# A dilated-attention and GEGLU kernel: weighted values in adjacent pairs, exponentials in PSUM, FFN norm statistics on ScalarE, and another order

## The chip, the cores and the metric

The kernel runs on one core of a Trainium2 chip. The metric is the device time of one execution in microseconds (us); less is better. A core has five engines that run side by side, each through its own list of instructions in the order in which they were written: TensorE (PE, with PEld for its weight loads), VectorE (DVE), ScalarE (ACT), GpSimd (POOL) and SyncE (SP, which here only starts DMAs). An instruction waits on semaphores for what other engines have to finish first, and whatever stands behind it on its engine waits with it.

## The reference

Two layers, each an attention block and a feed-forward block with a layer norm ahead of each, on 2048 positions of 512 channels. The two layers share their weights.

```python
x = A_x                                   # (1, 2048, 512)
for layer in range(2):
    x = x + attention(layernorm(x), wqkv, wo)
    x = x + ffn(layernorm(x), w_gate, w_up, w_down)

def attention(x, wqkv, wo):               # 32 heads of 16 channels
    q, k, v = split(x @ wqkv)
    idx = pos - 2 * arange(8)             # 8 positions, every second one backwards
    logits = q . k[idx] / 4               # masked where idx < 0
    return (softmax(logits) . v[idx]) @ wo

def ffn(x, w_gate, w_up, w_down):         # 1792 hidden channels
    return (gelu(x @ w_gate) * (x @ w_up)) @ w_down
```

## The kernel before

**Tiles and stages.** Since every second position is attended, even and odd positions never meet inside an attention block. The 2048 positions are cut into eight chunks of 256 positions of one parity, and each layer passes over the eight chunks, 16 chunk passes in all. For a chunk, `attention_inputs` norms the rows and makes q, k and v on PE (four projections of 24 matmuls each, line 1016), sends them to DRAM (`qkvd`), and `attention` fetches them back so that each partition holds two positions (`J` = 2) and the seven before them. Attention itself is vector work, for four groups of eight heads (`hg`), which are taken in two halves of two groups (`NG` = 2). fp32 accuracy is kept by splitting each operand into two fp16 parts and running three matmuls for each product.

**Attention on DVE.** For each head group, `prod` takes q times the eight attended keys (line 1100, 2048 products for each partition), line 1109 sums them over the 16 channels of a head into the logits `lg`. For each half, the maximum over the window is taken and subtracted (lines 1131, 1136), ACT takes the exponential in place in `lg` (line 1141), and the sum, its reciprocal and the scaling follow (lines 1146, 1150, 1155). Then, for each head group, `prod` takes the weights times the attended values (line 1166), in the order position, window place `w`, channel `c`, and line 1176 sums over the window:

```python
nc.vector.tensor_reduce(o.tile(), prod.rearrange("p j w c -> p j c w"), axis=AX.X, op=ALU.add)
```

The sum over `w` is the innermost one, so this instruction reads one 4-byte word and then jumps by 128 words (512 bytes) for the next. The result `o` (one buffer) is split on ACT and POOL (lines 931, 935) and transposed by a DMA into `ot` (one buffer).

**Feed-forward.** `feed_forward` multiplies `ot` by `wo` on PE (line 979, 24 matmuls of 512 columns), adds the residual on DVE (line 1214) and norms the rows: `norm` takes mean and variance on DVE (`bn_stats` and `bn_aggr`, lines 855 and 859), POOL makes scale and bias out of them in eight small instructions (lines 909 to 921), ACT applies them (line 968). After the split and the DMA transpose into `bx`, seven **units** follow. A unit is 48 gate and up matmuls into one of two PSUM buffers `pg` (line 979, weights `w_g` and `w_u`), a gelu on ACT (line 1267), a product on DVE (line 1275), three sums on POOL (lines 1286 to 1288), a cast on ACT (line 1296), a difference on POOL (line 1301), and then a **down unit** of 21 matmuls into the PSUM accumulator `pd` (line 1310). `down` uses the seven-product form of a 2x2 block multiplication, so `pd` holds seven blocks of 256 columns; after the seventh unit, DVE gathers them into the residual (line 1337, six instructions).

`pd` lies in a PSUM tile of eight such blocks, `pd_all`, four banks of two blocks each. Early in the kernel its two halves serve as two more `pg` buffers, until the nodes called `retire` take them back.

**What sets the order.** Nothing is issued in the order of the loops. Every operation is a node of a graph `g` with an engine, an assumed duration, the data that it reads and writes and a priority; `plan` places the nodes by a list schedule, and the instructions are then written in the order of their planned starts. Buffers are leased from pools (`Lease`, `Pool`), so the plan also decides which buffer a node gets. The priorities come from a table of some 70 numbers, `AT`. Semaphore waits are put in afterwards, by the layer that records the instructions, from the memory that they touch; it does not know the plan, and the plan does not know of waits that it adds for memory which two nodes merely share.

Of the kernel before, what the change touches and what calls it, by code (L numbers as in the profile page):

```python
# [13 lines left out]
ALU = mybir.AluOpType  # L14
# [38 lines left out]
    lq0=-6486.17, lq1=-3733.04, lf0=-475.32, lo=-1195.16, lf1=-292.25, ld=-286.77, pq0=-1258.2, pq1=2564.18,  # L53
    pf0=-676.71, po=-72.24, pf1=-123.32, pd=270.05, x0=-2156.6, first=54.86, tile=9.81, ahead=10.4, lead=445.97,
    norm=359.9, proj=149.42, half=24.02, row=-49.66, att=87.48, hg1=-5.5, hg2=11.94, kv=93.28, xl=185.47, gu=9.51,
    early=1, xin=225.5, wait=-0.0, zero=-300.31, dl=0, ds=0, pds=114.94, late_end=60.76, sp=1, fp=1, ng=2,
    hgk=1.38, vlag=20.87, hgv=54.57, retire=1.9, late=31.94, hold=0, dz=5, pdu=11.07, sf0=173.25, sf1=281.83,
    a1=-45.95, a2=-92.04, mx1=17.89, put=0, pt=6, fa=[0, 0], warm=7.7, xe=-394.02, mq1=-1270.4, queue=2.72,
    x1=-302.68, start=145.78, step=67.54, c1=53.56, c2=-58.19, c3=41.55, c4=-98.58, c5=152.01, c6=-107.83,
    c7=-23.55,  # L60
# [13 lines left out]
class Lease:  # L74
# [4 lines left out]
    def slots(self):  # L79

        p = self.pool
        return [i for i, h in enumerate(p.held) if h is None and self.only in (None, i)]
# [244 lines left out]
def dilated_attention_geglu(ctx: ExitStack, tc: tile.TileContext, x, wqkv, wo, wg, wu, wd, out):  # L327
# [18 lines left out]
    prod = sb.tile([P, JM, W, P], F32, name="prod")  # L346
    make_identity(nc, ident)
# [87 lines left out]
    P_lg = pool("lg", 2, [P, JM, W, AT["ng"] * HPG])  # L435
# [8 lines left out]
    P_pd = Pool("pd", [pd_all])  # L444
    P_pr = Pool("prod", [prod], fifo=False)

    for i, w in enumerate((w_g, w_u)):
        last = Lease(P_gh, only=i)
        w.raw_key = lambda k, w=w, last=last: (last, 0) if k == w.nb - 1 else (f"r{w.key}", k)
        g.add("SP", 0.001, lambda: None, w=[(last, 0)], get=[last], prio=-2000)  # L450

    retire = []
    for i in (2, 3):
        gone = Lease(P_pg, only=i, kept=True)
# [4 lines left out]
    def exponents(name, am, keys, prio):  # L459
# [3 lines left out]
        lease = Lease(P_pg)  # L463
# [227 lines left out]
    def prep_d(prio):  # L691
# [40 lines left out]
        for u in range(NU):  # L732
# [19 lines left out]
            for s in range(2):  # L752
                sc = Lease(P_sc) if s else Lease(P_bx, only=1)
# [86 lines left out]
    def norm(xs_of, prio, on="DVE", after=0.0):  # L840
# [12 lines left out]
        for j in range(J):  # L853
# [53 lines left out]
        else:  # L907

            op(lambda m, v, c: ts(c[V], v, EPS, None, op0=ALU.add), mvs, [V])
# [10 lines left out]
            op(lambda m, v, c: tt(c[HF], m, c[SC], op=ALU.mult), [SC], [HF])  # L920
            op(lambda m, v, c: ts(c[BI], c[HF], -1.0, None, op0=ALU.mult), [HF], [BI])
        return lease, lambda j: (view()[2][SC][:, j : j + 1], view()[2][BI][:, j : j + 1])

    def split_transpose(src, src_keys, nb, dst, w, get, prio, on="SP", after=()):
# [19 lines left out]
        pt = Lease(P_pg)  # L944
# [16 lines left out]
    def normed(x_of, norm_l, scale_bias, j, dst, w, get, prio, on="SP", keep=False, after=()):  # L961
        xn = Lease(P_sc) if keep else None
# [3 lines left out]
        def emit():  # L966
# [5 lines left out]
            get=[xn] if keep else [], prio=prio,  # L972
# [81 lines left out]
    def attention(l, c, T):  # L1054
# [7 lines left out]
        for first in range(0, HG, NG):  # L1062
# [23 lines left out]
            lg, mx = Lease(P_lg), Lease(P_mx)  # L1086
# [4 lines left out]
            mxb = lambda mx=mx: mx.tile().unsqueeze(2).to_broadcast([P, J, W, nh])  # L1091

            for hg in group:
# [3 lines left out]
                def qk(q=q, k=k):  # L1097
# [12 lines left out]
                        lgv()[:, :, :, heads], prod.rearrange("p j w (h d) -> p j w h d", d=DH), axis=AX.X, op=ALU.add  # L1110
# [6 lines left out]
            if t0 == 0:  # L1117
                g.add(
                    "DVE port", t_dve(nl),
                    lambda lgv=lgv, h=h: nc.vector.scalar_tensor_tensor(  # L1120
                        lgv(), lgv(), cst["s_log", h],
                        masks[J].unsqueeze(3).to_broadcast([P, J, W, nh]),
                        op0=ALU.mult, op1=ALU.add,
                    ),
                    r=[("s_log", h)], w=[(lg, 0)], prio=prio,
                )
                scale = 1.0
            sw = lambda lgv=lgv: lgv().rearrange("p j w h -> p j h w")
            g.add(
                "DVE", t_dvr(nl),  # L1130
# [302 lines left out]
```

## Time and profile before

| | |
|---|---|
| Time, median of three runs | 1322.2 us (1313.49 to 1324.21) |
| Profiled execution: time | 1320.53 us |
| Profiled execution: span from first to last instruction | 1318.7 us |
| Mean granted TensorE clock | 0.975 of full speed |
| PE busy | 1218.3 us (92%) |
| DVE busy | 1090.7 us (83%) |
| POOL busy | 799.6 us (61%) |
| ACT busy | 490.5 us (37%) |
| DMA, mean rate over the span | 133 GB/s |

The profile shows one execution. Each engine's busy time is the time in which one of its instructions was running, waits not counted. The span is 1.8 us shorter than the time of that execution, which lies 1.7 us under the median of the three runs. Lines such as L1176 are those of the kernel above; `o<-prod` says that `o` was written and `prod` read, by the program's names without buffer numbers.

### The profile page before, as it was taken

What the parts mean: (1) busy time and instruction counts of PE and PEld (TensorE: products, weight loads), DVE (VectorE), ACT (ScalarE), POOL (GpSimd) and SP (SyncE); (2) the same over time, 40 slices, a digit from 0 to 9 for tenths busy, and PEclk for the clock granted to TensorE, in tenths of its full rate; (3) what the DMA queues carried; (4) which work ended last, traced back from release to release, by engine and by line L of the source; (5) the groups of instructions that cost most, each with busy time, mean ns of one, the idle gap of its engine ahead of it and who ended that gap; (6) DMA issues with size and microseconds to landing.
All of it is one profiled execution on the core that took longest, in us unless ns stands there. A gap on an engine that the chain in (4) does not pass through costs nothing.

```text
span 1318.7 us, 23744 instructions
## 1 busy us (share of the span) xinstructions
PE 1218.3 (92%) x9722; PEld 957.6 (73%) x9722; DVE 1090.7 (83%) x964; ACT 490.5 (37%) x691; POOL 799.6 (61%) x855
## 2 busy tenths in 40 slices
PE   5689979999989999999999998989999999997997
PEld 2355548886867778687878766877888786886886
DVE  7999998899797778989889878788988997998221
ACT  5867243333332242334243324323332323333221
POOL 3334627766674747568585827766768565565543
PEclk7899989999999999999999998999999999999999
DMA  9889861335436334645436284334433434431100
GB/s 342 290 225 239 188 198 49 101 115 160 123 113 172 94 108 124 173 130 159 138 91 186 89 205 121 90 117 121 136 101 98 137 112 118 114 107 47 37 17 17
DMA packets 195789, 174.74 MB, mean 133 GB/s; under 512 B 101904, under 2 KB 162656, under 8 KB 195680
## 3 DMA queue, kind: packets, MB, share of 16 engines
q1 hardware_dynamic: 195680, 173.23, 45.2%
q8 instruction: 76, 1.25, 0.4%
q14 instruction: 33, 0.27, 0.1%
HBM read 115.87 MB, written 33.73 MB: 113 GB/s over the span
## 4 chain that ended last, share of the span: by engine, by line
PE 32%; DVE 30%; POOL 19%; issue 8%; DMA 7%; ACT 4%; SPq 1%; POOLq 0%; DVEq 0%; ACTq 0%
PE pg L979 17%; DVE o L1176 8%; PE pd L1310 8%; PE pg L1016 6%; DVE prod L1166 4%; POOL sc L1286 4%; DVE prod L1100 4%; POOL hl L935 3%; DVE x L1337 3%; DVE lg L1109 3%; POOL sc L1287 2%; POOL sc L1288 2%; POOL w_u L1301 2%; POOL w_g L1301 2%; POOL gh L1301 1%
## 5 line engine op out<-in xcount | busy, mean ns | idle before, releaser
L979 PE MATMUL pg<-bx,w_g 128*128 128x256 f16 x2688 | 331.7, 273 | 13.2 <-DVE sc L1275 13.1
L979 PE MATMUL pg<-bx,w_u 128*128 128x256 f16 x2688 | 331.0, 273 | 0.0
L979 PEld LDWEIGHTS <-w_g 128*128 128x128 f16 x2688 | 263.8, 98 | 46.2 <-issue 14.8
L979 PEld LDWEIGHTS <-w_u 128*128 128x128 f16 x2688 | 263.5, 98 | 31.0
L1016 PE MATMUL pg<-w_q,ax 128*128 128x512 f16 (+1 forms) x1536 | 264.3, 333 | 18.7 <-DMA ax<-hl 11.3
L1176 DVE TENSOR_REDUCE o<-prod 128x256 f32<-128x2048 f32 x64 | 236.9, 3702 | 18.1 <-POOL hl L935 16.8
L1016 PEld LDWEIGHTS <-ax 128*128 128x128 f16 x1536 | 152.3, 99 | 126.8 <-issue 18.1
L1275 DVE SCALAR_TENSOR_TENSOR sc<-pg,small,sc 128x512 f32<-128x512 f32 (+1 forms) x128 | 85.4, 677 | 134.1 <-ACT sc L1267 134.0
L935 POOL TENSOR_TENSOR hl<-o,hl 128x256 f16<-128x256 f32 x64 | 83.9, 1310 | 185.1 <-ACT hl L931 185.1
L1286 POOL TENSOR_TENSOR sc<-sc 128x256 f32<-128x256 f32 x112 | 122.3, 1092 | 96.3 <-DVE sc L1275 93.8
L1100 DVE TENSOR_TENSOR prod<-kv,q 128x2048 f32<-128x2048 f32 x64 | 165.0, 2577 | 3.0 <-DMA kv<-qkvd 2.7
L1166 DVE TENSOR_TENSOR prod<-kv,lg 128x2048 f32<-128x2048 f32 x64 | 163.1, 2548 | 0.6
L1109 DVE TENSOR_REDUCE lg<-prod 128x128 f32<-128x2048 f32 x64 | 145.9, 2279 | 1.0
L1267 ACT ACTIVATE sc<-pg,small 128x512 f32<-128x512 f32 (+1 forms) x128 | 79.3, 631 | 95.6 <-PE pg L979 91.8
L1310 PE MATMUL pd<-w_d,gh 128*128 128x256 f16 x798 | 97.4, 278 | 13.3 <-DVE x L1337 13.3
L1310 PE MATMUL pd<-w_d,w_u 128*128 128x256 f16 x777 | 93.7, 276 | 11.9 <-DVE x L1337 11.6
L979 PE MATMUL pg<-w_o,ot 128*128 128x512 f16 x384 | 88.4, 384 | 12.0 <-DMA ot<-hl 10.0
L1310 PEld LDWEIGHTS <-gh 128*128 128x128 f16 x798 | 79.5, 100 | 25.5 <-issue 14.5
L1288 POOL TENSOR_TENSOR sc<-sc 128x256 f32<-128x256 f32 x112 | 91.5, 817 | 8.8
L1310 PEld LDWEIGHTS <-w_u 128*128 128x128 f16 x777 | 76.9, 99 | 24.5 <-issue 12.5
L1310 PE MATMUL pd<-w_d,w_g 128*128 128x256 f16 x777 | 91.2, 272 | 3.2 <-DVE x L1337 3.1
L1301 POOL TENSOR_TENSOR gh<-sc,gh 128x896 f16<-128x896 f32 x38 | 76.5, 2014 | 28.3 <-ACT gh L1296 28.1
(111 smaller groups left out, 1347.8 us busy)
## 6 DMA issues: line engine op xcount, KB each, us to landing
kv<-qkvd SPq DMA_DIRECT2D x128, 576.0 KB, 3.9
qkvd<-sc SPq DMA_DIRECT2D x64, 384.0 KB, 3.3
q<-qkvd SPq DMA_DIRECT2D x64, 128.0 KB, 3.7
x<-in_A_x_dram SPq DMA_DIRECT2D x9, 512.0 KB, 5.0
xs<-x SPq DMA_DIRECT2D x8, 512.0 KB, 3.3
xa<-xs SPq DMA_DIRECT2D x16, 256.0 KB, 5.9
x<-xs SPq DMA_DIRECT2D x8, 512.0 KB, 4.3
xa<-in_A_x_dram SPq DMA_DIRECT2D x14, 256.0 KB, 4.1
```

The lines of the kernel that those rows point to most:

```text
L935: "POOL", t_pool(n), lambda: nc.gpsimd.tensor_sub(lo(), src(), hi()),
L979: nc.tensor.matmul(pt, a, b, start=i == 0, stop=i == n - 1)
L1016: nc.tensor.matmul(pt[:, lo:hi], a[:, i // 2, kt], part(h * KT + kt)[:, lo:hi], start=(i, kt) == (0, 0), stop=(i, kt) == (2, KT - 1),)
L1100: nc.vector.tensor_mul(prod, win, q.tile().unsqueeze(2).to_broadcast([P, J, W, P]))
L1109: lambda lgv=lgv, heads=heads: nc.vector.tensor_reduce(lgv()[:, :, :, heads], prod.rearrange("p j w (h d) -> p j w h d", d=DH), axis=AX.X, ...
L1166: nc.vector.tensor_mul(prod.rearrange("p j w (h d) -> p j w h d", d=DH), win, lg.tile()[:, :, :, heads].unsqueeze(4).to_broadcast([P, J, W ...
L1176: lambda o=o: nc.vector.tensor_reduce(o.tile(), prod.rearrange("p j w c -> p j c w"), axis=AX.X, op=ALU.add),
L1275: lambda sel=sel, h=h, pg=pg, g_of=g_of: nc.vector.scalar_tensor_tensor(g_of()[:, sel], pg.tile()[:, sel, JM * P : JM * P + N], cst["c_up" ...
L1286: tt(b[:, 4:6], b[:, 0:2], b[:, 3:4].to_broadcast([P, 2, P]), op=ALU.add)
L1288: tt(b[:, 1:3], b[:, 1:3], b[:, 0:4:3], op=ALU.subtract)
L1301: lambda blocks=blocks, gh_of=gh_of: nc.gpsimd.tensor_sub(gh_of()[:, 1], blocks(), gh_of()[:, 0]),
L1310: nc.tensor.matmul(pd.tile()[:, PD_AT[m]], gh_of()[:, a, G_AT[m]], wd_of(u, m, b), start=u == 0 and n == 0 and PD_AT[m] % 2 == 0, stop=u = ...
```

## The change

Line numbers of the changed kernel are some 32 to 36 higher: L1166 becomes L1199, L1176 becomes L1211, the exponential L1141 becomes L1173, the down unit L1310 becomes L1346.

- **Pairs.** The weighted values are written so that window places 2q and 2q+1 of a channel are neighbours (`paired`). The product is made in two instructions for each head group, one for each position `j`, and walks place pair, place in the pair, head, channel; so it writes every second word, first the even words of a stretch of 256 and then the odd ones. The sum reads two neighbouring words and then jumps by 256 words.
- **Logits** are kept with the window innermost, so the maximum reads `lg`, and the sum the exponentials, without jumps. The mask is applied in two instructions for each half instead of one.
- **Exponentials in PSUM.** ACT writes them to `ex`, one buffer, which is the eighth block of `pd_all`; the sum, the scaling in place and the weighted values read them there. Other users of the `pg` buffers than the q, k, v projections may no longer take the half of `pd_all` in which it lies (`WHOLE`).
- **FFN norm statistics on ACT.** For each of the two rows of a partition: a copy that also gives the sum, a multiplication of that sum by -1/D, and a square with that as its bias that also gives the sum of squares. POOL's list for an FFN norm is shorter by one instruction. The norms ahead of attention keep `bn_stats` on DVE.
- **Order.** Nearly all numbers of `AT` are others (`lead=445.97` becomes `lead=1721.82`, `step=67.54` becomes `step=134.57`), and some assumed durations.

```diff
+    paired = prod.rearrange("p j w c -> p j (w c)").rearrange("p j (q c t) -> p j q c t", c=P, t=2)
...
-    P_lg = pool("lg", 2, [P, JM, W, AT["ng"] * HPG])
+    P_lg = pool("lg", 2, [P, JM, AT["ng"] * HPG, W])
...
+    WHOLE = (0, 1, 2)
+    P_pe = Pool("pe", [pd_all[:, 7].rearrange("p (j h w) -> p j h w", j=JM, h=AT["ng"] * HPG)])
...
+        for j in range(J if into else 0):
...
+                lambda j=j, sums=sums, junk=junk: act(junk(), xs_of[j][1](), AF.Copy, accum_out=sums(0)),
...
+                lambda j=j, sums=sums: nc.scalar.mul(view()[1][:, j, 0:1], sums(0), -1.0 / D),
...
+                    junk(), xs_of[j][1](), AF.Square, bias=view()[1][:, j, 0:1], accum_out=view()[1][:, j, 1:2]
...
-                lambda lgv=lgv, scale=scale: nc.scalar.activation(lgv(), lgv(), AF.Exp, scale=scale),
-                r=[("s_log", h)], w=[(lg, 0)], prio=prio - 1000, table="exp",
+                lambda lgv=lgv, ex=ex, scale=scale: nc.scalar.activation(ex.tile(), lgv(), AF.Exp, scale=scale),
+                r=[("s_log", h), (lg, 0)], w=[(ex, 0)], get=[ex], prio=prio - 1000, table="exp",
...
-                    win = bass.AP(r.tensor, r.offset, [r.ap[0], [P, J], [P, W], [DH, HPG], [1, DH]])
+                    win = bass.AP(r.tensor, r.offset, [r.ap[0], [2 * P, W // 2], [P, 2], [DH, HPG], [1, DH]])
+                    by = ex.tile()[:, j, heads].rearrange("p h (q t) -> p q t h", t=2)
                     nc.vector.tensor_mul(
-                        prod.rearrange("p j w (h d) -> p j w h d", d=DH), win,
-                        lg.tile()[:, :, :, heads].unsqueeze(4).to_broadcast([P, J, W, HPG, DH]),
+                        paired[:, j].rearrange("p q (h d) t -> p q t h d", d=DH), win,
+                        by.unsqueeze(4).to_broadcast([P, W // 2, 2, HPG, DH]),
                     )
...
-                        o.tile(), prod.rearrange("p j w c -> p j c w"), axis=AX.X, op=ALU.add
+                        o.tile(), paired.rearrange("p j q c t -> p j c q t"), axis=AX.XY, op=ALU.add
...
-        nl, sb_of = norm(xt, T - 1000, "POOL" if AT["fp"] else "DVE")
+        nl, sb_of = norm(xt, T - 1000, "POOL" if AT["fp"] else "DVE", into=xns if AT["fs"] else None)
```

The rows below are the instructions of an engine as they stand in the program, each with the semaphores that it waits for (`PE_49` is raised by PE, `DVE_49` by DVE, `DMAHW...` by a DMA); a semaphore of the instruction's own engine is among them where it reads what that engine has just written.

On DVE, in the third chunk pass of the first layer, before: two head groups' weighted values (L1166) and their sums (L1176) among other work.

```order
L1155 TENSOR_TENSOR lg_108<-lg_108,mx_110 128x256
L1337 SCALAR_TENSOR_TENSOR x_90<-pd,small,x_90 128x2x256 [waits DVE_49]
L1166 TENSOR_TENSOR prod<-kv_105,lg_108 128x2048 [waits DMAHW3_49,DVE_49]
L1176 TENSOR_REDUCE o_112<-prod 128x256 [waits DVE_49,Pool_49]
L1100 TENSOR_TENSOR prod<-kv_104,q_107 128x2048 [waits DMAHW3_49,DMAHW0_49,DVE_49]
```

And after, at a like place: the scaling (L1187) and the weighted values (L1199), which read the exponentials in the tile `pd`, with a gather of `pd` (L1373) between them.

```order
L1187 TENSOR_TENSOR pd<-pd,mx_110 128x256 [waits DVE_49,PE_49]
L1199 TENSOR_TENSOR prod<-kv_104,pd 128x4x2x128 [waits DMAHW4_49,DVE_49]
L1199 TENSOR_TENSOR prod<-kv_104,pd 128x4x2x128 [waits PE_49]
L1373 SCALAR_TENSOR_TENSOR x_90<-pd,small,x_90 128x512 [waits PE_49]
L1211 TENSOR_REDUCE o_112<-prod 128x256 [waits DVE_49,Pool_49]
L1373 SCALAR_TENSOR_TENSOR x_90<-pd,small,x_90 128x2x256 [waits PE_49]
L1199 TENSOR_TENSOR prod<-kv_103,pd 128x4x2x128 [waits DMAHW1_49,DVE_49]
```

One product became two, and products and scaling now wait for PE: of these instructions and the sum of the exponentials 39 wait for a down unit, of the 32 exponentials on ACT 21 do, where before none did.

On PE, the first rows of a down unit before (`gh` is its input, made by ACT and POOL):

```order
L979 MATMUL pg_122<-bx_95,w_u 128x256
L1310 LDWEIGHTS gh [waits Activation_49]
L1310 MATMUL pd<-w_d,gh 128x256
L1310 LDWEIGHTS gh
L1310 MATMUL pd<-w_d,gh 128x256
L1310 LDWEIGHTS gh [waits Pool_49]
```

And after:

```order
L1011 MATMUL pg_122<-bx_95,w_u 128x256
L1346 LDWEIGHTS gh [waits Activation_49]
L1346 MATMUL pd<-w_d,gh 128x256 [waits DVE_49]
L1346 LDWEIGHTS gh
L1346 MATMUL pd<-w_d,gh 128x256
L1346 LDWEIGHTS gh [waits Pool_49]
```

The first matmul of the unit now waits for DVE too. Of the 2352 down matmuls 19 waited for DVE and none for ACT before, all for gathers; after, 69 wait for DVE and 7 for ACT, 62 of these for an instruction that uses the exponentials, 12 of them for one that stands at most ten instructions ahead in the program as written (30 for one at most forty ahead; a gate and up unit alone is 96).

On DVE before, behind the residual of the first chunk pass (L1214), the statistics of its FFN norm:

```order
L1214 SCALAR_TENSOR_TENSOR x_91<-pg_122,small,x_91 128x512 [waits PE_49,Activation_49]
L1214 SCALAR_TENSOR_TENSOR x_91<-pg_122,small,x_91 128x512
L855 BN_STATS nw_116<-x_91 128x6 [waits DVE_49] x2
L859 BN_AGGR nw_116<-nw_116 128x2 [waits DVE_49] x2
L1146 TENSOR_REDUCE mx_110<-lg_108 128x32 [waits Activation_49]
```

On ACT after, the same statistics for a later chunk pass, ahead of an exponential and a gelu:

```order
L859 ACTIVATE sc_101,nw_116<-x_91 128x512 [waits DMAHW4_49,DMAHW3_49,DVE_49]
L859 ACTIVATE sc_102,nw_116<-x_91 128x512 [waits DVE_49]
L868 ACTIVATE nw_116<-nw_116 128x1 [waits Activation_49] x2
L859 ACTIVATE sc_101,nw_116<-x_91,nw_116 128x512 [waits Activation_49]
L859 ACTIVATE sc_102,nw_116<-x_91,nw_116 128x512 [waits Activation_49]
L1173 ACT_TABLE_LOAD [waits DVE_49]
L1173 ACTIVATE pd<-lg_108,small 128x256 [waits PE_49]
L1303 ACT_TABLE_LOAD [waits PE_49]
```

The statistics left DVE and stand on ACT, six instructions for a chunk pass. Over the whole program ACT's table loads go from 54 to 60, and the first gate product on DVE (L1275, now L1311) has six sums over the window ahead of it instead of seven.

More of the change, by code (lines that the diff above doesn't have):

```diff
@@ L81, in slots @@
         p = self.pool
-        return [i for i, h in enumerate(p.held) if h is None and self.only in (None, i)]
+        return [i for i, h in enumerate(p.held) if h is None and (self.only is None or i in self.only)]
     def tile(self):
@@ L971, in normed @@
             "ACT", t_act(D, 2), emit, r=[x_of[0], (norm_l, 4), (norm_l, 5)], w=[key],
-            get=[xn] if keep else [], prio=prio,
+            get=[xn] if keep and not held else [], prio=prio,
         )
```

137 lines of the change are left out of this document (82 added, 55 removed).

## The prediction

> **What bounds the kernel now.** I begin with the page: the span, the engines' shares, and the chain of work that ended last.
>
> ```profile
> span 1318.7 us, 23744 instructions
> PE 1218.3 (92%) x9722; PEld 957.6 (73%) x9722; DVE 1090.7 (83%) x964; ACT 490.5 (37%) x691; POOL 799.6 (61%) x855
> ...
> PE 32%; DVE 30%; POOL 19%; issue 8%; DMA 7%; ACT 4%; SPq 1%; POOLq 0%; DVEq 0%; ACTq 0%
> PE pg L979 17%; DVE o L1176 8%; PE pd L1310 8%; PE pg L1016 6%; DVE prod L1166 4%; POOL sc L1286 4%; DVE prod L1100 4%; POOL hl L935 3%; DVE x L1337 3%; DVE lg L1109 3%; POOL sc L1287 2%; POOL sc L1288 2%; POOL w_u L1301 2%; POOL w_g L1301 2%; POOL gh L1301 1%
> ```
>
> PE is busy for 92% of the span, yet only a third of the chain lies on it: DVE and POOL hold 49% of it. The largest single DVE piece is L1176, the sum over the window, with 8%. Next, busy time by stage: the start up to the first gate matmuls, the long middle, and the end in which no attention is left.
>
> ```profile
> core 0: us, PE busy (x) PEld busy (x) DVE busy (x) ACT busy (x) POOL busy (x), PEclk, DMA share, GB/s
> 0.00:200.00 200.00, 157.94 (x904) 91.06 (x905) 184.13 (x240) 117.64 (x183) 77.53 (x120) 0.91 0.83 245
> 200.00:1200.00 1000.00, 958.04 (x7941) 779.37 (x7939) 869.35 (x682) 347.44 (x474) 662.95 (x669) 0.99 0.43 123
> 1200.00:1319.00 119.00, 102.28 (x882) 87.22 (x880) 37.18 (x43) 25.45 (x35) 59.13 (x67) 0.95 0.09 26
> ```
>
> PE stands idle for 42.1 us in the start, 42.0 in the middle and 16.7 at the end, 100.8 us in all. The change takes no matmul away, so that sum is about the most that it can gain. DVE is at 92% in the start and 87% in the middle: two engines are near their limits at once, and a cut on one of them is paid only until the other is met.
>
> **The change part by part.** The rows that price DVE's share, mean ns of one behind the busy time:
>
> ```profile
> L1176 DVE TENSOR_REDUCE o<-prod 128x256 f32<-128x2048 f32 x64 | 236.9, 3702 | 18.1 <-POOL hl L935 16.8
> L1166 DVE TENSOR_TENSOR prod<-kv,lg 128x2048 f32<-128x2048 f32 x64 | 163.1, 2548 | 0.6
> L1109 DVE TENSOR_REDUCE lg<-prod 128x128 f32<-128x2048 f32 x64 | 145.9, 2279 | 1.0
> L1214 DVE SCALAR_TENSOR_TENSOR x<-pg,small,x 128x512 f32<-128x512 f32 x32 | 22.4, 742 | 7.1 <-PE pg L979 7.1
> L855 DVE BATCH_NORM_STATS2 nw<-x 128x6 f32<-128x512 f32 x34 | 21.7, 679 | 0.0
> L1155 DVE TENSOR_TENSOR lg<-lg,mx 128x256 f32<-128x256 f32 x32 | 19.0, 592 | 0.5
> L1131 DVE TENSOR_REDUCE mx<-lg 128x32 f32<-128x256 f32 x32 | 18.6, 580 | 0.4
> L1146 DVE TENSOR_REDUCE mx<-lg 128x32 f32<-128x256 f32 x32 | 18.5, 578 | 15.2 <-ACT lg L1141 14.9
> L859 DVE BATCH_NORM_AGGREGATE nw<-nw 128x2 f32<-128x6 f32 x64 | 10.1, 173 | 0.2
> L1120 DVE SCALAR_TENSOR_TENSOR lg<-lg,small,mask 128x256 f32<-128x256 f32 x8 | 6.5, 810 | 0.0
> L704 DVE TENSOR_TENSOR w_d<-w_d 128x512 f32<-128x512 f32 x5 | 3.4, 681 | 0.0
> ...
> L1166 DVE TENSOR_TENSOR prod<-kv,lg x64: 2257/2292/3976, 92.9 to 1210.3; 128x2048 f32<-128x2048 f32 x64
> L1176 DVE TENSOR_REDUCE o<-prod x64: 3567/3704/3777, 95.5 to 1217.0; 128x256 f32<-128x2048 f32 x64
> ```
>
> The last two rows give min, median and max. From L704 (512 elements, 681 ns) and the median of L1166 (2048, 2292 ns): 1.049 ns an element and 144 ns for the instruction. L1109 fits this with neighbouring words (2279 ns). L1176 reads as many and never takes less than 3567: (3704 - 144)/2048 = 1.74 ns an element, at a jump of 512 bytes for every word. L1131 jumps by 64 bytes: (580 - 144)/256 = 1.70. So the jump costs 0.7 ns a word, and L1176 pays it in all 64 runs: it isn't waiting for another engine.
>
> - **The sum over the window (L1211)** reads two neighbours and then jumps by 256 words. No row shows such a read; the bounds are 2279 ns (L1109) and 3702 (as now). I take the lower one, since each jump now serves two words: 64 x 1.42 = -91 us.
> - **The weighted values (L1199)**: 128 instructions of 1024 elements. L1214 against L704, both 512 elements, shows 61 ns for a PSUM operand. At the full rate one takes 144 + 61 + 1024 x 1.049 = 1279 ns, two 2558 against 2548 now: +1 us. No row shows a write that steps by two words. If that costs what the jumping read costs, one takes 205 + 1024 x 1.74 = 1.99 us: +91 us. A gain under 2548 is excluded, as the elements are as many and none has ever run faster than 1.04. I take the full rate; the step is 8 bytes, while the jumps that cost are 64 and 512, but this is the least certain number here.
> - **Smaller DVE terms.** FFN statistics leave: 32 x (679 + 173) = -27 us. The maximum and the sum without jumps, 413 and 474 ns: -5 and -3. The scaling with a PSUM operand 474: -4. The mask in halves, 16 x 278 ns instead of 8 x 810: -2.
>
> Together -131 us, DVE 1091 to 960; with the dear write, 1050.
>
> [...]
>
> ACT and POOL:
>
> ```profile
> L573 ACT ACTIVATE sc<-w_d 128x512 f32<-128x512 f32 x14 | 8.6, 618 | 0.2 <-DMA qkvd<-sc 0.2
> L741 ACT ACTIVATE w_d<-w_d,small 128x512 f32<-128x512 f32 x10 | 6.4, 711 | 0.0
> L573 ACT ACTIVATION_READ_ACCUMULATOR sc<-w_d 128x1 f32 x18 | 3.4, 189 | 0.0
> L1267 ACT ACT_TABLE_LOAD x27 | 34.6, 1283 | 43.0 <-PE pg L979 32.4 <-issue 10.2
> L921 POOL TENSOR_SCALAR nw<-nw 128x2 f32<-128x2 f32 x31 | 16.1, 518 | 2.7
> ```
>
> - **FFN statistics on ACT.** A row costs 618 + 189 for the copy with its sum, some 190 for the small product (the accumulator read is the nearest row), 711 + 189 for the square with a pointer operand: 1.9 us, 61 us in all. Six more table loads make 8. ACT ends near 560 us, 42%, and no engine-time limit is near. Latency is what counts: for a chunk pass 3.8 us instead of 1.7 on DVE, less 0.5 on POOL for the instruction that goes (L921), so 1.6 us longer from residual to normed rows, 26 us over 16 passes if nothing covered it. The next rows show the cover.
>
> ```profile
> 302.04 4.71 PE L979 MATMUL pg<-w_o,ot 128*128 128x512 f16 x21 [1.01 <-DMA ot<-hl]
> ...
> 317.36 11.86 PE L1016 MATMUL pg<-w_q,ax 128*128 128x512 f16 x72
> 329.06 1.47 PE L979 MATMUL pg<-bx,w_g 128*128 128x256 f16 x12
> ```
>
> Between the output projection (ending at 306.8) and the first gate matmul of that pass, PE has 22 us of other matmuls without a gap worth naming. In the new program three to five gate-and-down pairs of the previous pass stand there. I price the statistics at 0; without that cover, 26.
>
> - **The shared bank.** This is what the change adds without saying so. The exponentials lie in the tile of the down accumulator, and the program now carries a wait both ways: a down unit waits for the last DVE or ACT instruction on the exponentials ahead of it (62 waits), and 39 DVE and 21 ACT instructions wait for a whole down unit. What it costs is bounded by the other side's duration: 1.28 us for a running product, and a down unit of 21 matmuls:
>
> ```profile
> 285.15 2.46 PE L1310 MATMUL pd<-w_d,gh 128*128 128x256 f16 x21
> ...
> PE pd L1310 <- DVE x L1337: 28.0, 16, 5.6
> DVE sc L1275 <- ACT sc L1267: 134.0, 42, 8.8
> PE pg L979 <- DVE sc L1275: 13.1, 8, 4.8
> ```
>
> On PE: from 0 to 62 x 1.28 = 79 us. PE stands in order, so gate and up matmuls queue behind a waiting down unit. Where a gate unit (5.2 us) lies between, the product should be over; 12 waits stand close behind their product, and I take 12 x 1.28 = +15 us. The kind of wait is there already: 16 waits of a down unit for gathers, 28.0 us, 1.75 each. On DVE: from 0 to 39 x 2.46 = 96 us. Behind the waiting product stand sums, queries of the next group and the gate products L1275, for which PE waits 13.1 us now. Its cover is the 131 us that DVE has just been given, so I take 0; without that cover it is 96 us on an engine as busy as before.
>
> - **The order.** Queues keep their kinds of work: SP starts the same loads, with w_d's last loads behind the first stores of q, k, v. Projections are spread singly between gate and down units instead of in blocks of two to five, and run out earlier; PE's total stays. POOL gets no new kind of work. I price this at 0 and leave it to the range.
>
> **The sum.** DVE's cut counts where it is on the chain: L1176 holds 8% of 1318.7, 105 us, and loses 1423/3702 of it, 38%: -41 us. The other 40 us of cut DVE work lie in pieces too small for the chain's list, or off it; 0, and at most -40. PE's waits give +15. Net -26: 1320.5 (the profiled execution, 1.7 under the median, well inside the spread of 10.7 of the three runs) becomes **1294 us**. The end of that case: 1271 (the waits at 0 and a part of the remaining cut paid) to 1308 (half the chain's gain lost).
>
> **The rivals.**
> 1. *The stepped write costs like a jump* (L1199), and the result is slower. DVE is then at 1050, and with the 96 us of waits above what it has now. The chain's L1166 (4%, 53 us) grows by 3.97/2.55, +29; the waits come on the path with DVE's share of the chain, 30% of 96, +29: -41 + 29 + 15 + 29 = +32, 1353 us. It decides from where DVE's total meets the old one: (1091 - 960 - 96)/128 = 0.27 us above 1.28, so at 1.55 us for one L1199. For it: L1176 and L1131 both show jumps punished; against it: the step is far smaller.
> 2. *The bank locks PE to DVE.* All 62 waits cost a product: -41 + 79, 1358 us. It decides from 41/62 = 0.66 us a wait. For it: the planner knows nothing of these waits; against it: 50 of the 62 stand farther off.
> 3. *PE and POOL take the chain over.* PE at 96% of the middle and POOL's sums, differences and their waits are as long as before; the gain on DVE is slack: 1310 to 1325.
> 4. *The pairs do not help the read*: L1211 stays near 3.7. DVE gets 40 us at most, the waits remain: 1320.5 + 15, about 1336.
> 5. *More is gained*: the whole cut is paid and waits stay small: 1320.5 - 81 = 1240, at most; 1240 to 1270.
>
> **How the numbers follow.** Forecast 0.43; rival 1: 0.17; 2: 0.08; 3: 0.17; 4: 0.05; 5: 0.10. Within 1% of 1322.2 (1309 to 1335, about what a measurement of this kernel can tell from no change) lie rival 3 and a little of 4; so faster 0.55, same 0.19, slower 0.26. The range must take in the forecast, rivals 3 and 4, the nearer part of 5 and the milder half of 1: 1255 to 1346.
>
> **What would show it.** L1211 near 2.28 us and L1199 near 1.28 (rival 1 from 1.55); DVE's busy time near 960; ACT near 560; PE's waits for L1199 in the list of waits near 15 us in all, not 80; PE idle in the middle down from 42 us; sums L1211 no longer among the first of the chain. I am wrong if the stepped write is dear, if down units wait for products by more than 0.66 us each, or if PE's idle time stays at 100 us though DVE's cut is there.

## The result, and the profile after

The changed kernel takes 1302.1 us in the median (four runs, 1299.56 to 1303.3) against 1320.0 us before: a ratio of 0.9866 (95% interval 0.982 to 0.9912), or 18 us less. The forecast was 1294 us.

The page of the changed kernel, its head and its chain:

```profile
span 1300.3 us, 23949 instructions
PE 1215.1 (93%) x9722; PEld 955.8 (74%) x9722; DVE 937.8 (72%) x972; ACT 541.5 (42%) x857; POOL 684.7 (53%) x839
...
PE 66%; DVE 16%; DMA 5%; POOL 4%; ACT 4%; issue 4%; SPq 0%; ACTq 0%; DVEq 0%; POOLq 0%
PE pg L1011 37%; PE pd L1346 18%; PE pg L1048 8%; DVE prod L1199 4%; PE pd L1048 3%; DVE o L1211 2%; DVE x L1373 2%; DVE lg L1141 1%; DVE prod L1132 1%; DVE sc L1311 1%; DVE small L564 1%; POOL hl L966 1%; DMA kv<-qkvd 1%; DMA ax<-hl 1%; DMA bx<-hl 1%
```

DVE's busy time fell by 153 us and POOL's by 115, though POOL has only 16 instructions fewer; the span fell by 18. Two thirds of the chain now lie on PE. The same stages as before, busy time by engine:

```profile
0.00:200.00 200.00, 159.74 (x905) 91.52 (x906) 163.34 (x238) 116.23 (x191) 57.15 (x118) 0.91 0.80 241
200.00:1200.00 1000.00, 964.32 (x8005) 784.66 (x8003) 755.99 (x707) 401.33 (x629) 580.37 (x667) 0.99 0.43 125
1200.00:1301.00 101.00, 91.05 (x816) 79.59 (x814) 18.47 (x27) 23.99 (x39) 47.15 (x54) 0.97 0.05 17
```

PE's idle time is 40.3, 35.7 and about 9 us, 85.2 in all (span less busy time) against 100.4 before. So the change, with its large cut on DVE, took 15 us off PE's idle time and 3 us off its busy time. The groups that the prediction priced (mean ns of one behind the busy time), and three that it did not, the first two of them of the kernel before:

```profile
L1136 DVE TENSOR_TENSOR lg<-lg,mx 128x256 f32<-128x256 f32 x32 | 28.1, 879 | 0.5
L1100 DVE TENSOR_TENSOR prod<-kv,q 128x2048 f32<-128x2048 f32 x64 | 165.0, 2577 | 3.0 <-DMA kv<-qkvd 2.7
```

```profile
L1132 DVE TENSOR_TENSOR prod<-kv,q 128x2048 f32<-128x2048 f32 x64 | 156.6, 2447 | 9.2 <-DMA kv<-qkvd 6.1 <-issue 2.2 <-DVE x L1373 0.4
L1199 DVE TENSOR_TENSOR prod<-kv,pd 128x1024 f32<-128x1024 f32 x128 | 153.0, 1218 | 31.8 <-PE pd L1346 28.5 <-ACT sc L1068 2.3
L1211 DVE TENSOR_REDUCE o<-prod 128x256 f32<-128x2048 f32 x64 | 146.1, 2282 | 18.1 <-POOL hl L966 15.2
L1168 DVE TENSOR_TENSOR lg<-lg,mx 128x256 f32<-128x256 f32 x32 | 18.0, 561 | 0.2
```

The sum over the window is at 2282 ns, the lower of its two bounds, and the product whose write steps by two words is at 1218 ns, under the 1279 that I had estimated with 1.049 ns an element. Last, what PE waited for: of its list of waits the rows in which the exponentials or a gather hold it (us in all, times, longest):

```profile
PE pd L1346 <- DVE prod L1199: 18.7, 18, 1.8
PE pd L1346 <- DVE x L1373: 8.9, 10, 1.3
...
PE pd L1346 <- ACT pd L1173: 6.0, 3, 3.2
...
PE pd L1048 <- DVE mx L1178: 4.3, 3, 2.8
PE pd L1048 <- DVE prod L1199: 2.9, 1, 2.9
...
PE pd L1346 <- DVE mx L1178: 2.2, 3, 1.3
...
PE pd L1048 <- ACT pd L1173: 0.7, 1, 0.7
...
PE pd L1346 <- DVE pd L1187: 0.4, 1, 0.4
```

Down units waited 25 times for something done to the exponentials, 27.3 us in all, and projections (L1048), which use the other buffers in that tile early in the kernel, 7.9 us more. The row of L1373 is that of the gathers.

### The profile page after: what moved, and what is told of

The parts are those of the page before. It is cut to its first block, busy times and chain, and to the rows that moved or that the text cites. A ratio compares the mean times of both kernels' runs of the same rounds, so it can differ in the third digit from the quotient of the medians.

```text
span 1300.3 us, 23949 instructions
## 1 busy us (share of the span) xinstructions
PE 1215.1 (93%) x9722; PEld 955.8 (74%) x9722; DVE 937.8 (72%) x972; ACT 541.5 (42%) x857; POOL 684.7 (53%) x839
## 4 chain that ended last, share of the span: by engine, by line
PE 66%; DVE 16%; DMA 5%; POOL 4%; ACT 4%; issue 4%; SPq 0%; ACTq 0%; DVEq 0%; POOLq 0%
PE pg L1011 37%; PE pd L1346 18%; PE pg L1048 8%; DVE prod L1199 4%; PE pd L1048 3%; DVE o L1211 2%; DVE x L1373 2%; DVE lg L1141 1%; DVE prod L1132 1%; DVE sc L1311 1%; DVE small L564 1%; POOL hl L966 1%; DMA kv<-qkvd 1%; DMA ax<-hl 1%; DMA bx<-hl 1%
## 5 line engine op out<-in xcount | busy, mean ns | idle before, releaser
L1011 PEld LDWEIGHTS <-w_g 128*128 128x128 f16 x2688 | 263.4, 98 | 35.0 <-issue 2.5
L1048 PEld LDWEIGHTS <-ax 128*128 128x128 f16 x1536 | 152.2, 99 | 128.1 <-issue 27.5
L1322 POOL TENSOR_TENSOR sc<-sc 128x256 f32<-128x256 f32 x112 | 108.7, 970 | 236.1 <-DVE sc L1311 235.9
L1048 PE MATMUL pg<-w_q,ax 128*128 128x256 f16 (+1 forms) x1176 | 200.3, 328 | 0.5 <-DMA ax<-hl 0.2
L1311 DVE SCALAR_TENSOR_TENSOR sc<-pg,small,sc 128x512 f32<-128x512 f32 (+1 forms) x128 | 85.6, 679 | 141.1 <-ACT sc L1303 137.6
L1199 DVE TENSOR_TENSOR prod<-kv,pd 128x1024 f32<-128x1024 f32 x128 | 153.0, 1218 | 31.8 <-PE pd L1346 28.5
L1132 DVE TENSOR_TENSOR prod<-kv,q 128x2048 f32<-128x2048 f32 x64 | 156.6, 2447 | 9.2 <-DMA kv<-qkvd 6.1
L1211 DVE TENSOR_REDUCE o<-prod 128x256 f32<-128x2048 f32 x64 | 146.1, 2282 | 18.1 <-POOL hl L966 15.2
L1141 DVE TENSOR_REDUCE lg<-prod 128x128 f32<-128x2048 f32 x64 | 145.8, 2278 | 1.0
L1373 DVE SCALAR_TENSOR_TENSOR x<-pd,small,x 128x512 f32<-128x512 f32 x96 | 70.6, 741 | 60.4 <-PE pd L1346 56.5
L1346 PE MATMUL pd<-w_d,gh 128*128 128x256 f16 x798 | 94.3, 272 | 13.4 <-DVE prod L1199 7.8
L1346 PE MATMUL pd<-w_d,w_g 128*128 128x256 f16 x777 | 94.6, 278 | 11.5 <-DVE prod L1199 4.8
L1346 PE MATMUL pd<-w_d,w_u 128*128 128x256 f16 x777 | 91.3, 272 | 13.2 <-DVE prod L1199 6.1
L966 POOL TENSOR_TENSOR hl<-o,hl 128x256 f16<-128x256 f32 x64 | 52.7, 824 | 95.4 <-ACT hl L962 94.6
L1346 PEld LDWEIGHTS <-gh 128*128 128x128 f16 x798 | 77.9, 98 | 25.6 <-issue 15.0
L1346 PEld LDWEIGHTS <-w_g 128*128 128x128 f16 x777 | 77.2, 99 | 23.9 <-issue 13.3
L1346 PEld LDWEIGHTS <-w_u 128*128 128x128 f16 x777 | 76.0, 98 | 24.2 <-issue 15.3
L1337 POOL TENSOR_TENSOR w_g<-sc,w_g 128x896 f16<-128x896 f32 x37 | 76.4, 2064 | 30.7 <-ACT w_g L1332 30.7
```

Source lines behind the costliest of these rows:

```text
L1011: nc.tensor.matmul(pt, a, b, start=i == 0, stop=i == n - 1)
L1048: nc.tensor.matmul(pt[:, lo:hi], a[:, i // 2, kt], part(h * KT + kt)[:, lo:hi], start=(i, kt) == (0, 0), stop=(i, kt) == (2, KT - 1),)
L1132: nc.vector.tensor_mul(prod, win, q.tile().unsqueeze(2).to_broadcast([P, J, W, P]))
L1141: lambda lgv=lgv, heads=heads: nc.vector.tensor_reduce(lgv()[:, :, heads].rearrange("p j h w -> p j w h"), prod.rearrange("p j w (h d) -> ...
L1199: nc.vector.tensor_mul(paired[:, j].rearrange("p q (h d) t -> p q t h d", d=DH), win, by.unsqueeze(4).to_broadcast([P, W // 2, 2, HPG, DH]),)
L1211: lambda o=o: nc.vector.tensor_reduce(o.tile(), paired.rearrange("p j q c t -> p j c q t"), axis=AX.XY, op=ALU.add),
```

## The experiments

All twelve were timed beside runs of the kernel before on the same chip, whose median was 1316.1 us for e1 to e4 and 1318.1 for the others. Differences between two experiments are therefore taken from their ratios, times 1318 us; the expectations on record reckon with medians, which gives 1 to 4 us more or less.

| run | what it is | median us | ratio to before (95%) |
|---|---|---|---|
| changed kernel | | 1302.1 | 0.9866 (0.982 to 0.9912) |
| e1 | `pd` in two tiles | 1251.8 | 0.951 (0.9481 to 0.9539) |
| e2 | exponentials in SBUF | 1286.0 | 0.9774 (0.9742 to 0.9806) |
| e3 | no pairs | 1353.3 | 1.0269 (1.0225 to 1.0313) |
| e4 | no pairs, exponentials in SBUF | 1336.8 | 1.0159 (1.0125 to 1.0193) |
| e5 | two tiles, no pairs | 1291.1 | 0.9805 (0.9766 to 0.9843) |
| e6 | two tiles, shared half first | 1269.8 | 0.9639 (0.9606 to 0.9673) |
| e7 | statistics on DVE, new plan | 1331.5 | 1.0105 (1.0066 to 1.0144) |
| e8 | whole change, old table | 1351.2 | 1.0266 (1.023 to 1.0303) |
| e9 | two tiles, exponentials in SBUF | 1265.9 | 0.9597 (0.9556 to 0.9639) |
| e10 | kernel before, two tiles | 1308.3 | 0.9924 (0.9902 to 0.9946) |
| e11 | statistics on DVE, same order | 1303.9 | 0.9891 (0.9851 to 0.9932) |
| e12 | two tiles, statistics on DVE, same order | 1254.5 | 0.9521 (0.9472 to 0.9569) |

Except in e6, e7 and e8 every engine keeps the order of the kernel it is made from. My theory was that PE is the bound and pays for the shared tile; the main rival, that DVE and POOL hold the chain and the waits only move.

### e1: the accumulator in two tiles

The semaphores are set by tile: a down unit waited at its first matmul, which writes block 0, for readers of block 7. With two tiles it waits at its 13th.

```diff
-    pd_all = ps.tile([P, 8, HD], F32, name="pd")
+    pd_half = [ps.tile([P, 4, HD], F32, name=f"pd{i}") for i in range(2)]
...
-                            pd.tile()[:, PD_AT[m]], gh_of()[:, a, G_AT[m]], wd_of(u, m, b),
+                            pd.tile()[PD_AT[m] // 4][:, PD_AT[m] % 4], gh_of()[:, a, G_AT[m]], wd_of(u, m, b),
```

> The changed kernel in its own order, with the PSUM tile of the down accumulator cut into two tiles of four blocks. The exponentials share a tile with blocks 4 to 6 only, so a down unit waits for their readers at its 13th matmul and not at its first. In the changed kernel PE's waits for products, exponentials and their sums ahead of down units were 18.7 + 6.0 + 2.2 = 26.9 us. Theory A (PE is the bound, and such a wait costs what it lasts): the mean wait of 1.04 us is shorter than 12 matmuls (1.3 us), so most of them go, and the time falls by 15 to 25 us, to 1277 to 1287. Rival B (PE is held by the chain through DVE and POOL, the waits only move): within 6 us of 1302.

Measured: 1251.8 us, 47 us less than the changed kernel (0.951 against 0.9866), below both theories and nearly twice the length of the waits. Of the 50 us between the two spans, 38 are PE's idle time and 12 its busy time. First the page's head and chain, then the stages, then what is left of the waits:

```profile
span 1250.4 us, 23954 instructions
PE 1202.9 (96%) x9722; PEld 953.4 (76%) x9722; DVE 930.7 (74%) x972; ACT 542.7 (43%) x857; POOL 692.9 (55%) x839
...
PE 85%; DVE 10%; DMA 2%; issue 2%; POOL 1%; ACT 1%; SPq 0%; DVEq 0%; ACTq 0%; POOLq 0%
```

```profile
0.00:200.00 200.00, 167.36 (x995) 99.71 (x996) 168.20 (x245) 124.41 (x197) 69.13 (x123) 0.91 0.80 241
200.00:1200.00 1000.00, 992.28 (x8336) 815.14 (x8334) 753.60 (x715) 408.42 (x648) 600.20 (x693) 1.00 0.43 125
```

```profile
PE pd L1346 <- DVE prod L1199: 3.6, 3, 2.4
...
PE pd L1346 <- ACT pd L1173: 2.1, 2, 1.9
```

PE is idle for 7.7 us of the middle's 1000, not 35.7, and 85% of the chain lie on it: this kernel is bound by PE. Down units still wait six times at the exponentials (6.5 us, once for the scaling, L1187), each time at the 13th matmul. The waits for gathers (L1373), 8.9 us in the changed kernel, are gone from the list as well, since a gather reads only one half of `pd`. So e1 loosens two kinds of waits; e2 and e9 part them.

### e2 and e9: exponentials in SBUF, with one tile and with two

```diff
-                lambda ...: nc.scalar.activation(ex.tile(), lgv(), AF.Exp, scale=scale),
+                lambda ...: nc.scalar.activation(lg.tile(), lgv(), AF.Exp, scale=scale),
```

The sum, the scaling and the weighted values then read and write `lg.tile()`; the lease of `ex` is kept, so that the plan stays as it is. e9 has the two tiles of e1 besides.

> The changed kernel in its own order, but the exponentials are taken in place in the logits' SBUF tile. All waits between down units and exponentials are gone; in exchange the products L1199 read two SBUF operands again. In the two traces POOL's instructions run up to 2 us longer when they start beside a product of two SBUF operands: 111 us beside L1100 and 74 us beside L1166 before, 72 us beside L1132 and none beside L1199 after. Theory A (the shared bank is the dear part, POOL has slack): POOL's busy time rises by some 70 us from 685, yet the time falls by 15 to 25 us, as with the split tile. Rival B (POOL's stalls and L1199's own stalls matter as much): 1300 to 1315, no gain over the changed kernel.

> Exponentials in the SBUF tile (as in the run with 1286.0 us), and the down accumulator in two tiles all the same; no instruction stands elsewhere. Nothing waits for exponentials then, and what the two tiles change is the waits between down units and gathers alone (17.1 us of PE's waits for L1373 in that run). Theory A (part of the 50 us that the two tiles gave were waits for gathers): 1270 to 1280. Rival B (all of the 50 were waits for the exponentials): 1283 to 1289. What is left between this one and 1251.8 is what the PSUM operand brings with two tiles.

Measured: 1286.0 and 1265.9 us. In e2 the median lies just inside theory A's range (1277 to 1287), but by the ratios the gain is 12 us, less than the 15 to 25 that it gave; rival B is out. POOL's busy time rose by 84 us to 768, as theory A had it. e9 came out faster than its theory A (1270 to 1280). From e2 to e9, 23 us: these go with the waits between gathers and down units, 17.1 us on PE's side in e2's list, though projections that use the two halves early in the kernel are parted too:

```profile
PE pd L1346 <- DVE x L1373: 17.1, 11, 4.8
```

From the changed kernel to e2, -12 us: the waits for exponentials go, and so does what the PSUM operand gives to POOL and to the products. Call that the relief. From e9 to e1, -11 us: the relief comes, and what is left of those waits with it, so the relief is worth at least 11. If it is worth the same with one tile, and the waits for gathers too, the waits for exponentials cost 12 + 11 = 23 us more with one tile than with two. That is an estimate, since PE's waits for gathers were 8.9 us in the changed kernel and 17.1 in e2. The relief shows in POOL's split of `o` (the same 64 instructions, first the changed kernel, then e2) and in the products, 1541 ns in e2 against 1218; no run parts POOL's share from that of the products:

```profile
L966 POOL TENSOR_TENSOR hl<-o,hl 128x256 f16<-128x256 f32 x64 | 52.7, 824 | 95.4 <-ACT hl L962 94.6 <-DMA x<-in_A_x_dram 0.6
```

```profile
L966 POOL TENSOR_TENSOR hl<-o,hl 128x256 f16<-128x256 f32 x64 | 69.5, 1086 | 67.5 <-ACT hl L962 67.3
...
L1199 DVE TENSOR_TENSOR prod<-kv,lg 128x1024 f32<-128x1024 f32 x128 | 194.0, 1541 | 1.1
```

### e3, e4 and e5: the pairs undone

```diff
-                    win = bass.AP(r.tensor, r.offset, [r.ap[0], [2 * P, W // 2], [P, 2], [DH, HPG], [1, DH]])
+                    win = bass.AP(r.tensor, r.offset, [r.ap[0], [P, W], [DH, HPG], [1, DH]])
...
-                        o.tile(), paired.rearrange("p j q c t -> p j c q t"), axis=AX.XY, op=ALU.add
+                        o.tile(), prod.rearrange("p j w c -> p j c w"), axis=AX.X, op=ALU.add
```

e3 does this in the changed kernel, e4 with e2's edit, e5 with e1's.

> The changed kernel in its own order, with the weighted values written in the old order (place, channel) and the sum reading with jumps again; the exponentials stay in PSUM. L1211 goes back to 3.70 us, DVE's busy time from 938 to about 1029. Theory A (in the changed kernel PE is the bound, DVE at 72% has slack): slower by 5 to 20 us, 1307 to 1322. Rival B (the pricing of the prediction, 8% of the chain times 38%): slower by 41 us or more, 1343.

> The changed kernel in its own order, with both undone: no pairs, exponentials in place in SBUF. What is left of the change is the order, the statistics on ScalarE and the logits' layout. Theory A (the gain is that of pairs and PSUM; the order by itself brings none): about the time of the kernel before, 1315 to 1335. Rival B (the gain is that of the order and of the statistics on ScalarE): near 1302. If this one and the one without pairs differ, the difference is what PSUM costs or brings while DVE is full.

> The kernel with the accumulator in two tiles, but without pairs (old write order, jumping sum); everything else and the order as there. With one tile the pairs were worth 1353.3 - 1302.1 = 51 us. Theory A (DVE's length reaches PE only through the waits at the shared tile): with these waits gone the pairs are worth much less, 1255 to 1275. Rival B (DVE's length reaches PE by other ways too, and the parts add up): 1295 to 1310.

Measured: the pairs are worth 53 us in the changed kernel (1.0269 - 0.9866), 51 with exponentials in SBUF, 39 with two tiles. My theory for e3, that DVE at 72% had slack, fell; the pricing by the chain (41 us) was the nearer one. e4, at 1336.8 us, goes with theory A, just above its range. Of e3, the page's line of the engines, the groups of sums and products, and the largest entry in PE's list of waits:

```profile
PE 1236.0 (91%) x9722; PEld 964.4 (71%) x9722; DVE 1026.1 (76%) x972; ACT 542.0 (40%) x857; POOL 684.7 (51%) x839
```

```profile
L1211 DVE TENSOR_REDUCE o<-prod 128x256 f32<-128x2048 f32 x64 | 237.1, 3705 | 13.3 <-POOL hl L966 10.3
L1199 DVE TENSOR_TENSOR prod<-kv,pd 128x1024 f32<-128x1024 f32 x128 | 152.7, 1215 | 32.0 <-PE pd L1346 29.6 <-ACT sc L1068 1.2
```

```profile
PE pd L1346 <- DVE prod L1199: 35.5, 21, 3.8
```

The sum falls back to 3705 ns, while the product without the step takes 1215 ns against 1218 with it. DVE is busy for only 76% of that span and still holds PE: its share of the whole says little where DVE, ACT and POOL hand an operand on and PE stands in order. e5, at 1291.1 us, lies just under rival B's range and far from theory A's. It does not settle how much of the pairs' worth goes through the waits at the tile, since down units wait there for the exponentials for 28.4 us, against 6.5 in e1. e2 and e4 do: nothing waits for exponentials in either, and the pairs still bring 51 us. A longer sum on DVE reaches PE by other ways too.

### e6: the shared half first

```diff
-            order = [5, 4, 3, 2, 7, 6, 1]
+            order = [7, 6, 1, 5, 4, 3, 2]
```

> The kernel with the accumulator in two tiles, but a down unit begins with the three blocks that share the exponentials' tile: PE waits again at its first matmul, while DVE and ACT have to wait only for the 9th matmul of 21 and not for the last. Theory A (it is PE's wait that is dear): the 50 us come back in good part, 1280 to 1300. Rival B (it is DVE's and ACT's waits for the unit's end that are dear): 1245 to 1255.

Measured: 1269.8 us, 17 us over e1, between the two theories. PE's waits at the tile came back,

```profile
PE pd L1346 <- DVE prod L1199: 9.9, 9, 2.4
PE pd L1346 <- ACT pd L1173: 7.5, 7, 1.8
```

while DVE's products, sums and scalings waited less for down units, 29.5 us against 34.0 in e1. The time grew all the same, so PE's side costs. That not all came back fits e9, by which about half of the 47 us went with the gathers, whose waits stay away here. The last unit's parts are planned in another order, so a few us may be the plan's.

### e7 and e11: FFN norm statistics on DVE

e7 sets `fs=0` in the table, and the order is planned anew. e11 puts other instructions into the same places:

```diff
-                lambda ...: act(junk(), xs_of[j][1](), AF.Copy, accum_out=sums(0)),
+                lambda j=j: nc.vector.bn_stats(view()[0][:, j], xs_of[j][1]()),
...
-                lambda ...: nc.scalar.mul(view()[1][:, j, 0:1], sums(0), -1.0 / D),
+                lambda j=j: nc.vector.bn_aggr(view()[1][:, j], view()[0][:, j]),
```

> The changed kernel with the FFN norm statistics on DVE as before (32 bn_stats, 32 bn_aggr), the rest of the change kept; the order is planned anew from the same table, so it differs in places. Theory A (the prediction's 0 for the statistics): within 10 us of 1302. Rival B (the statistics' latency on ScalarE costs): faster, near 1302 - 26 = 1276. Rival C (the 27 us of DVE are missed): 1312 to 1330.

> The changed kernel with the FFN norm statistics on DVE, but without a new plan: bn_stats and bn_aggr stand where the copy and the multiplication stood, the square is left out, POOL has its eighth instruction again; all else is in the same order. Theory A (the prediction's 0 for the statistics; the 1331.5 us of the run with a new plan were the plan's): 1292 to 1312. Rival B (DVE misses the 27 us while it is tied to PE by the shared tile): 1317 to 1332.

Measured: 1331.5 us, just above rival C's range, and 1303.9 us, within theory A's. With the order kept the statistics are worth 3 us (0.9891 against 0.9866, the intervals overlap): priced at 0, rightly. The other 28 us of e7, which has the same work, go with the new plan; a single wait of 16.2 us, for a transposed input, stands in PE's list:

```profile
PE pg L1011 <- DMA bx<-hl: 17.5, 2, 16.2
```

### e8: the change with the old table

```diff
-    lead=1721.82, norm=577.77, proj=-72.68, half=166.44, ...
+    norm=359.9, proj=149.42, half=24.02, ..., lead=445.97, ...
```

> The whole change but its order: the table of the kernel before, with pairs, exponentials in the shared PSUM tile and statistics on ScalarE. The four runs before this one, in the new order, give -51 us for the pairs, -34 for the PSUM operand (1286.0 - 1251.8) and +50 for the shared tile; from the kernel before that would be 1316 - 35 = 1281 if the order were worth nothing. Theory A (the new order brings nothing by itself): 1275 to 1290. Rival B (the new order is what makes the shared tile bearable): 1305 to 1340.

Measured: 1351.2 us, slower than the kernel before and above rival B's range. Not as rival B meant it, though: its stages and PE's longest wait put most of the loss in the start.

```profile
0.00:200.00 200.00, 123.09 (x725) 74.48 (x726) 164.54 (x228) 114.69 (x182) 63.56 (x112) 0.82 0.68 215
200.00:1200.00 1000.00, 950.59 (x7754) 759.87 (x7752) 739.96 (x695) 388.79 (x611) 572.96 (x637) 0.99 0.43 128
```

```profile
PE pg L1048 <- DVE w_q L525: 32.9, 3, 28.2
```

PE is idle for 77 us of the first 200, 35 more than before, and one wait for a prepared weight lasts 28.2 us. The old numbers seem not to suit the changed graph; the run therefore does not price the new order alone. e4 comes nearer to that: new order, logits' layout, products in two halves and statistics on ScalarE, without pairs and without PSUM, are 21 us slower than the kernel before.

### e10: two tiles in the kernel before

> The kernel before with its down accumulator in two tiles, and nothing else; the order is the same instruction for instruction. PE there waited 28.0 us, 16 times, for gathers ahead of down units. Theory A (these waits cost about what they last): 1293 to 1308. Rival B (DVE and POOL hold the chain there, and PE waits for them elsewhere): 1312 to 1322.

Measured: 1308.3 us, ratio 0.9924: 10 us faster, at the upper edge of theory A (1308). PE's waits for gathers fell from 28.0 us to 7.6, but the wait of the output projection for its transposed input rose from 10.0 to 17.8:

```profile
PE pg L979 <- DMA ot<-hl: 17.8, 7, 4.7
...
PE pd L1310 <- DVE x L1337: 7.6, 3, 4.2
```

So of 20 us of waits that went, 8 came back at another place within this list, and half of the 20 reached the end.

### e12: two tiles and statistics on DVE

The edits of e1 and e11 together.

> The same with the accumulator in two tiles (1251.8 us with the statistics on ScalarE). Theory A (statistics priced at 0 there too; six table loads and 46 us of ACT less, 27 us of DVE more): 1247 to 1260. Rival B (DVE's 27 us are missed at about the rate at which the pairs' 91 us gave 39): 1260 to 1270.

Measured: 1254.5 us, within theory A's range and 1 us from e1 by the ratios. The place of the statistics does not matter there either. e1 is the fastest kernel of the case, ahead of both kernels that were compared.

## Why the prediction was right, and where it was not

1302.1 lies in the forecast's own range (1271 to 1308), and the sign was right. The sum was -41 + 15 = -26 us; what was measured is this chain of runs, from the kernel before by ratios: new order with layout, half products and statistics +21 (e4), pairs -51 (e4 to e2), exponentials in the shared PSUM tile +12 (e2 to the changed kernel), together -18. The sign and the pairs were forecast for the right reason; that the total came within 8 us of the sum is in part luck: the order cost 21 us that the sum did not have, the pairs and the PSUM operand together 13 less than it had.

- **The pairs: right in mechanism, 10 us too small.** L1211 came out at 2282 ns as chosen. Its share of the chain times its cut gave 41 us, and 39 to 53 were measured. The runs that undo the pairs change nothing else, so the other 40 us of cut DVE work, priced at 0, do not explain the difference; of those 40, e11 puts the statistics at 3 us, and no run parts the rest. DVE's cut was 153 us, not 131: three groups that read two SBUF operands before were held up less, the products (L1166 to L1199 10 us, L1100 to L1132 8 us) and the subtraction (L1136 to L1168, 879 to 561 ns, 10 us). The shortest subtractions took 415 ns before and 359 after, so about half of the mean of 879 was time in which they stood still, and no jump went away.
- **The stepped write: rightly taken as free.** 1218 ns against 1215 without the step (e3). My 1279 put the PSUM operand too high. I had excluded a gain under 2548 ns for the two halves, and they take 2436: 2548 was L1166's mean, while its median, in my own rows, was 2292. The 256 ns between the two are the hold-up beside POOL, of which the products with the PSUM operand show none (1187 to 1261 ns). Rival 1 is out.
- **The shared tile: the right kind of wait, too small a price.** 18 waits for L1199 at 1.04 us came close to the 12 at 1.28 that I took. The 7 others of down units, at exponentials, sums and a scaling (8.6 us), and those of projections (7.9 us) were left out. In time these waits cost about 23 us (e2, e9, e1), where the term was 15. My 0 for DVE's side was not tested apart; DVE waited 26 times for down units at these instructions, 44.2 us in all. Rival 2's point, 0.66 us for each of 62 waits or 41 us in all, was not reached.
- **What was missing: POOL.** With the PSUM operand (L1166 to L1199) POOL and the product no longer hold each other up (POOL's extra time beside them went from about 70 us to none), at least 11 us to the good (e9 to e1). I had written that POOL gets no new kind of work and left it at 0; its busy time fell by 115 us, of which e2 gives 84 back. This gain took back about half of what the waits cost, and so the term for the exponentials, +15, is close to the measured +12 by luck: one term was too small and the other was left out.
- **The order at 0: wrong by about 20 us**, as far as e4 can tell it from the logits' layout, which saves DVE time, and from the halved products. It cancelled against the pairs' and POOL's larger gains. With pairs and PSUM undone the new order is slower than the old one.
- **The statistics at 0: right** (e11, e12). Rival 3 described the end state correctly (PE holds 66% of the chain) but not the time; rivals 4 and 5 did not come. Of what I named as proof, L1211 has 2% of the chain, PE's idle time in the middle went from 42.0 to 35.7 us, and DVE ended at 938 us (960 forecast), ACT at 541.5 (560). PE's idle time as a whole went from 100 to 85 us, less than the net 26 that I forecast.

## What to carry to other kernels

A tile is what the semaphores saw here: exponentials and down blocks, which never overlap in it, waited for each other all the same (27.3 us on PE's side, 44.2 on DVE's), and cutting the tile (no instruction moved) brought 47 us, where the whole change brought 18. Price a shared resource from both sides: the move to PSUM cost about 23 us of waits and gave at least 11 by ending a hold-up between DVE and POOL. And after a change to a scheduled graph, undo its parts with the order kept; a new plan alone moved the time by 28 us in e7.

## What the runs showed of the hardware that I had not expected

**In these traces POOL and a DVE instruction of two SBUF operands stood still for each other.** Rows of the kernel before, on the timeline (start and length in us):

```profile
504.39 2.26 DVE L1166 TENSOR_TENSOR prod<-kv,lg 128x2048 f32<-128x2048 f32 x1
504.46 2.77 POOL L1286 TENSOR_TENSOR sc<-sc 128x256 f32<-128x256 f32 x1 [2.19 <-DVE nw L859]
```

The sum on POOL, 728 ns in the median, starts 0.07 us after the product and ends 0.58 us after it. Adding up what POOL's instructions took beyond their usual time, by the DVE instruction they overlapped most: before, about 110 us beside L1100 and 70 beside L1166, 2 beside L1176, which has one operand; after, about 70 beside L1132 and none beside L1199; in e2, 75 beside L1199 again. DVE stood still too, where POOL was first:

```profile
380.89 1.89 POOL L1301 TENSOR_TENSOR w_g<-sc,w_g 128x896 f16<-128x896 f32 x1
...
380.96 2.10 DVE L1136 TENSOR_TENSOR lg<-lg,mx 128x256 f32<-128x256 f32 x1
```

The shortest L1136 takes 415 ns. This one starts 0.07 us after POOL's and ends 0.28 us after it. All 22 products L1166 that took over 2442 ns (150 above the median) started while an instruction of POOL was running (so did 10 of the 42 others). With the PSUM operand 59 of the 128 products started so, and none is long (min, median and max in ns, the changed kernel and then e2):

```profile
L1199 DVE TENSOR_TENSOR prod<-kv,pd x128: 1187/1216/1261, 99.7 to 1153.8; 128x1024 f32<-128x1024 f32 x128
```

```profile
L1199 DVE TENSOR_TENSOR prod<-kv,lg x128: 1194/1320/2909, 98.6 to 1139.1; 128x1024 f32<-128x1024 f32 x128
```

**PE's busy time was not fixed.** The same 9722 matmuls kept PE busy for 1236.0 us at a mean granted clock of 0.963 (e3), 1224.5 at 0.971 (e4), 1215.1 at 0.978 (changed kernel) and 1202.9 at 0.985 (e1), in the order of PE's idle time (118, 110, 85, 48 us). So from the changed kernel to e1 38 us of idle time were saved and 12 us of busy time with them. The extra lies mostly in the down matmuls, ahead of which PE waits: of the 33 us between e3 and e1, 18 are theirs (295.3 us of L1346 against 276.9), and 4 those of the gate and up matmuls (664.1 against 660.0). No run shows that idle time causes the lower clock, or the clock the longer busy time; e8 has 136 us of idle time and a clock of 0.968 but only 1213.1 us of busy time: its clock is lowest in the start (0.82), where PE stands idle most.
